# A softmax moved between two weight roundings, two late transposes and a store queue in an FFT filter + soft mixture + gated MLP kernel

## The chip, the cores and the metric

The kernel runs on one core of one Trainium2 chip. The metric is the device time of one execution in microseconds (us). The engines named below are TensorE (PE; PEld is its weight load), VectorE (DVE), ScalarE (ACT), GpSimd (POOL) and SyncE (SP). SP, ACT and POOL also issue DMAs (written SPq, ACTq, POOLq in the trace). Each engine runs its own instructions in program order, so an instruction that waits holds up everything behind it on that engine.

## The reference, cut to what matters

```python
X = np.fft.rfft(x, axis=1)                     # x: 8 x 3072 x 256
y = np.fft.irfft(X * (filt_r + 1j*filt_i)[None], n=3072, axis=1)   # -> 24576 tokens x 256
logits = y @ phi                               # 32 slots: 8 experts x 4
d = exp(logits - logits.max(0)); d /= d.sum(0) + 1e-09      # over all tokens
slot_input = (d.T @ y).reshape(8, 4, 256)
slot_out[e] = relu(slot_input[e] @ w1[e]) @ w2[e]           # F = 1024
c = exp(logits - logits.max(1)); c /= c.sum(1) + 1e-09      # over the 32 slots
z = c @ slot_out                               # 24576 x 256
g = z @ w_gate;  out = (g / (1 + exp(-g)) * (z @ w_val)) @ w_out    # hidden 1536
```

## The kernel before

**Three stages.** phase1 (0 to about 392 us of the profile) does the filter, the logits and the dispatch sums batch by batch; transition (to about 418 us) runs the eight experts on the 32 slots and multiplies the result into the gate and value weights; phase2 (to the end) walks 576 items, each of which makes G and V for 128 hidden units of 512 tokens (L964, L965), silu and product (L967, L973), a split into a rounded part and a remainder (L980, L981), and the projection to the output (L992, L996).

**Units of phase1.** A step is one half (128 of 256 channels) of one batch, so there are 16 steps; each has 6 units, written (step, u), 96 in all, numbered i. In a unit TensorE makes X (L258), DVE multiplies it by the filter into P and Q (L262, L263), POOL adds these into yt (L271, L273; the very last one on DVE). Two units later tail_ops transposes that yt through PSUM (T, L283, one buffer), and ACT copies it to y (L284); for odd u phi_pair multiplies two units by phi (L, L291), and DVE or ACT adds that to lts. For the next step s1_chunk makes s on TensorE (L230), DVE turns it (sg, L238), ACT spreads it into b (L247), which X reads.

**Chains.** When a batch is through, its generator chain(b) is advanced by pump once in each unit (twice in the last ten): transposes (L354), inverse transform (L364), a turn (L374), logits lg (L391, L398), store of the logits (L404), maximum, exponential (L422, L428), a second transform (L443, L455, L468) and the dispatch sum (L477). The chain of batch 7 (last) runs after the last unit with that of batch 6 (written g7 and g6), advanced by hand.

**Side work.** aside advances one list of generators, once or twice a unit: conv rounds the gate, value and output weights in 36 chunks (raw load L566, ACT L579 to L582, DVE L584, POOL L586 and L588, store L589), then first_weights makes the combining softmax of batch 0 in two halves G: load of the stored logits (lgf, L601), maximum (mx, L605), POOL subtraction (L606), exponential (L608), sum and reciprocal (sm, L611 to L613), POOL product (L614), turn (ctf, L617), rounding (chf, L620), remainder (L622), two stores to cd (L624). Its tiles and those of the raw weights are the same two buffers, taken in turn; half 1 can't load before a tile of half 0 has been stored. In phase2 build(b) does the same for batches 1 to 7 (L909 to L936).

**Queues.** Almost all loads and stores go out on SP in program order. A DMA of SP or ACT takes the next of eight semaphores (lanes; order calls them DMAHW0 to 7) and waits until the DMA eight before it has landed; those of POOL have lanes of their own (DMASW). While the last units run, the weights w1 are loaded by ACT's queue (L134), w2 by SP's (L743), then wv, the weights c4 (L891) and wo (L897).

**Ramp of phase2.** Item i makes G and V, then projects an item some places back. Up to item 11 load_out splits the output weights of one f: ACT copies a rounded part (L953), DVE subtracts the remainder (L954); proj of that f needs both. The gate and value weights for later f are put in place by 16 small DMAs (L871), half of them on POOL.

Of the kernel before, what the change touches and what calls it, by code (L numbers as in the profile page):

```python
# [12 lines left out]
ALU = mybir.AluOpType  # L13
# [4 lines left out]
NB, SEQ, D, E = 8, 3072, 256, 32  # L18
NEXP, SPE, FE, FF = 8, 4, 1024, 1536
NJ, NP, NR = 24, 96, 32  # L20
NF = FF // 128
# [4 lines left out]
CONV_AT = 14  # L26
# [53 lines left out]
def spectral_softmoe_glu_kernel(  # L80
# [17 lines left out]
    nc = tc.nc  # L98
    pe, dve, act, pool = nc.tensor, nc.vector, nc.scalar, nc.gpsimd
# [37 lines left out]
    def phase1():  # L137
        with ExitStack() as c1:
# [23 lines left out]
            yt = {}  # L162
            ytr = {}
# [108 lines left out]
                eng = dve if (step, u) == (2 * NB - 1, 5) else pool  # L272
                eng.tensor_tensor(out=y[:, :, 1, :], in0=Q[:, :, 0, :], in1=Q[:, :, 1, :], op=ALU.add)  # L273

            def tr_unit(step, u):
                b, h = divmod(step, 2)
                k = (6 * b + u - 6 * NB) % NY
                if h == 0:
                    yt[b, u] = yp[(k >= 2) + (k >= NY - 6)].tile([128, 4, D], F32, tag=f"y{k}", name="y")
                t = ytr[step, u // 2][:, u % 2].rearrange("p g r m -> p g (r m)")  # L280
                ps = ps_t.tile([128, 4, 128], F32, tag="T", name="T")
                for g in range(4):
                    pe.transpose(out=ps[:, g, :], in_=t[:, g, :], identity=ident)  # L283
                act.copy(yt[b, u][:, :, h * 128:(h + 1) * 128], ps)  # L284

            def phi_pair(step, q):
                b, h = divmod(step, 2)
                ps = ps_l.tile([128, 2, 128], F32, tag="L", name="L")
                t = ytr.pop((step, q)).rearrange("p u g r m -> p u g (r m)")
                for g in range(4):  # L290
                    pe.matmul(  # L291
                        out=ps[32 * g:32 * g + 32],
                        lhsT=phi_sb[:, h, :],
                        rhs=t[:, :, g, :],
                        tile_position=(0, 32 * g),
                    )
                if h == 0 and q == 0:
                    lts_t[b] = chp.tile([128, 3, 2, 128], F32, tag="lts", name="lts")
                dst = lts_t[b][:, q]
                if h == 0:  # L300
                    act.copy(dst, ps)
                else:
                    dve.tensor_tensor(out=dst, in0=dst, in1=ps, op=ALU.add)
# [4 lines left out]
            def chain(b, last):  # L308
# [92 lines left out]
                yield  # L401
                for h in range(2):
                    for g in range(2):
                        nc.sync.dma_start(  # L404
                            out=lgd[b].rearrange("(n h) g e k -> h g n e k", h=2)[h, g],
                            in_=lg[h][64 * g:64 * g + 48],
                        )
# [143 lines left out]
            def flat(a):  # L551
                return a.rearrange("(p a) f -> p (a f)", p=128)

            def conv():


                cw = 256
                chunks = [(i, c) for i in range(3) for c in range(FF * D // 128 // cw)]
                raws = {}

                def load(n):
# [86 lines left out]
                turn_filters(0, q)  # L648
            pool.tensor_scalar_mul(nyq, nyq, 0.5)
            dve.memset(expo, 0.0)  # L650
            side = [conv(), first_weights()]
            todo = []
            gens, ready = [], []
            units = [(s, u) for s in range(2 * NB) for u in range(6)]
# [16 lines left out]

            def tail_ops(i):
                if 0 <= i - 2 < len(units):
                    tr_unit(*units[i - 2])
                    s, u = units[i - 2]
                    if u % 2:
                        phi_pair(s, u // 2)
                    if s % 2 and u == 5:
                        ready.append((s // 2, chain(s // 2, s // 2 == NB - 1)))

            def aside():
                if next(side[0], 0) == 0 and len(side) > 1:
                    side.pop(0)

            for i, (s, u) in enumerate(units):
# [30 lines left out]
                    kept(1)  # L716
                if i == CONV_AT - 4 or i >= CONV_AT:
                    aside()
            wt = bp[1].tile([128, 3, FE], F32, tag="b", name="w")
            load_w1(nc.sync, 6, ((0, wt[:, 0]), (1, wt[:, 1])))  # L720
            load_w1(nc.sync, 7, ((1, wt[:, 2]),))
            for i in range(len(units), len(units) + 2):
                tail_ops(i)
            (_, g6), (_, g7) = gens + ready
            for g in (g7, g7, g7, g6, g7, g6, g7, g7, g6, g7, g6, g6):
                next(g, None)
            for _ in g7:
                pass
# [5 lines left out]
    def transition():  # L734
# [33 lines left out]
        for e in (6, 7, 0):  # L768
            load_w2(e)
        flat_load(wg, wd[0], 128)  # L770
        for e in (1, 2, 3, 5, 4):
            load_w2(e)
        flat_load(wv, wd[1], 128)

# [170 lines left out]
    def phase2(later):  # L945
# [5 lines left out]
        def load_out(f):  # L951
            st = wo[f][:, 1, :].bitcast(F32)
            act.copy(wo[f][:, 0, :], st)  # L953
            dve.tensor_tensor(out=wo[f][:, 1, :], in0=st, in1=wo[f][:, 0, :], op=ALU.subtract)  # L954

        items = [(b, q, G, f) for b in range(NB) for q in range(3) for G in range(2) for f in range(NF)]
        hb, hhi, hlo, acc, sb2 = {}, {}, {}, {}, {}
# [65 lines left out]
        for i in range(len(items) + LAG):  # L1023
            if i < len(items):
                b, q, G, f = items[i]
                if q == 0 and G == 0 and f == 0 and b:
                    for _ in gen:
                        pass
                    gen = build(b + 1) if b + 1 < NB else iter(())
                gv(i)  # L1030
            while todo and todo[0] <= i - lag(i):
                proj(todo.pop(0))
            if i < len(items):
                gate(i)
            if i < NF:
                load_out(i)
            if 0 <= i - 1 < len(items):
                split(i - 1)
            if i % 4 == 1:
                next(gen, None)  # L1040

    with tc.manual_schedule():
# [35 lines left out]
```

## Time and profile before

| | |
|---|---|
| median of three runs | 1502.65 us (1501.77, 1502.65, 1505.04) |
| the profiled execution | 1503.74 us |
| span of its trace | 1501.9 us (1.84 us of its time lie outside the span) |
| busy in the span | PE 1442.1, DVE 1158.6, ACT 962.7, POOL 232.9 us |

The times below are us from the start of the span. A row of the trace gives start, duration, engine, line, what is written and read, and in brackets the idle time of the engine before it and what ended that. The share of busy PE, 96%, is an average: phase2 and the middle of phase1 are nearly full, the last units of phase1 are not, so a change is to be read in the stage where it acts.

### The profile page before, as it was taken

How to read it: one execution, taken by the hardware profiler on the slowest of the kernel's cores; microseconds unless marked ns; L12 is line 12 of the kernel's file. 1: busy time of each engine (PE TensorE's matmuls, PEld its weight loads, DVE VectorE, ACT ScalarE, POOL GpSimd, SP SyncE). 2: the span in 40 equal slices, each digit the busy share in tenths (PEclk: the TensorE clock that was granted, in tenths of full speed). 3: DMA queues.
4: the chain of work that ended last, by engine and by line, in shares of the span. 5: the costliest groups of instructions: out<-in, count | busy, mean ns of one | idle time of the engine just before them, and what ended most of it. 6: DMA issues, size and time to landing. Idle time of an engine off the chain costs nothing.

```text
span 1501.9 us, 25182 instructions
## 1 busy us (share of the span) xinstructions
PE 1442.1 (96%) x9562; PEld 1152.8 (77%) x9562; DVE 1158.6 (77%) x1906; ACT 962.7 (64%) x1839; POOL 232.9 (16%) x299
## 2 busy tenths in 40 slices
PE   4899999986899999999999999999999999999998
PEld 2566666654468888888888888888888888888887
DVE  2788888874288878878887897888779778877775
ACT  2476666653277667766766776676676667666665
POOL 0466666652010000000000000000000000000000
PEclk9999999998999999999999999999999999999999
DMA  9978888855940310130121112111210310220011
GB/s 223 158 117 159 160 146 151 142 157 196 355 100 15 71 39 15 35 73 16 29 64 32 29 36 50 40 29 43 53 29 15 71 39 17 50 48 22 22 29 28
DMA packets 88248, 116.42 MB, mean 78 GB/s; under 512 B 8928, under 2 KB 65120, under 8 KB 88000
## 3 DMA queue, kind: packets, MB, share of 16 engines
q1 hardware_dynamic: 81072, 102.76, 31.6%
q10 hardware_dynamic: 6800, 11.54, 2.6%
q8 instruction: 75, 1.23, 0.4%
q0 software_dynamic: 256, 0.52, 0.2%
q14 instruction: 45, 0.37, 0.1%
HBM read 68.13 MB, written 34.60 MB: 68 GB/s over the span
## 4 chain that ended last, share of the span: by engine, by line
PE 85%; DVE 7%; DMA 4%; issue 2%; ACT 2%; POOL 0%; SPq 0%; ACTq 0%; DVEq 0%; POOLq 0%
PE o L992 35%; PE o L996 18%; PE V L965 9%; PE G L964 9%; PE X L258 4%; PE s L230 2%; PE T L283 2%; DVE sg L238 2%; PE c L477 1%; DVE Q L263 1%; DVE P L262 1%; PE L L291 1%; DMA wo<-wod 1%; DMA fraw<-in_filt_i_dram 1%; ACT b L247 1%
## 5 line engine op out<-in xcount | busy, mean ns | idle before, releaser
L992 PE MATMUL o<-wo,hi 128*128 128x512 f32 x2304 | 831.2, 395 | 0.0
L996 PE MATMUL o<-wo,lo 128*128 128x256 f32 x2304 | 644.6, 280 | 0.2 <-DVE lo L981 0.2
L967 ACT ACTIVATE s<-G 128x512 f32<-128x512 f32 x576 | 345.1, 599 | 318.1 <-PE G L964 314.6
L973 DVE TENSOR_TENSOR h<-V,s 128x512 f32<-128x512 f32 x576 | 395.0, 686 | 169.5 <-ACT s L967 168.8
L992 PEld LDWEIGHTS o<-wo,hi 128*128 128x128 f32 x2304 | 432.0, 187 | 103.4
L996 PEld LDWEIGHTS o<-wo,lo 128*128 128x128 f32 x2304 | 433.6, 188 | 25.9 <-DVE lo L981 0.6
L981 DVE TENSOR_TENSOR lo<-h,hi 128x512 fp32r<-128x512 f32 x576 | 417.1, 724 | 0.1
L980 ACT CAST hi<-h 128x512 fp32r<-128x512 f32 x576 | 354.7, 616 | 12.4 <-DVE h L973 9.1
L965 PE MATMUL V<-c,v 128*128 128x512 f32 x576 | 227.3, 395 | 1.9 <-DVE h L973 1.7
L964 PE MATMUL G<-c,g 128*128 128x512 f32 x576 | 228.0, 396 | 0.8 <-DMA g<-gl 0.6
L258 PEld LDWEIGHTS X<-fwd,b 128*128 128x128 f32 x768 | 97.1, 198 | 61.0 <-issue 41.2
L964 PEld LDWEIGHTS G<-c,g 128*128 128x128 f32 x576 | 108.1, 188 | 26.8 <-issue 1.1
L238 DVE STREAM_TRANSPOSE sg<-s 128x1024 f32<-128x1024 f32 x64 | 79.3, 1242 | 60.2 <-PE s L230 58.8
L258 PE MATMUL X<-fwd,b 128*128 128x128 f32 x768 | 113.7, 293 | 4.6 <-DVE Q L263 3.1
L965 PEld LDWEIGHTS V<-c,v 128*128 128x128 f32 x576 | 108.6, 189 | 3.7 <-DVE h L973 2.7
L911 POOL TENSOR_TENSOR lg<-lg,mx 96x1024 f32<-96x1024 f32 x7 | 16.9, 2418 | 581.8 <-DVE mx L909 581.8
L247 ACT COPY b<-sg 128x768 f32<-128x768 f32 x64 | 58.8, 922 | 67.4 <-DVE sg L238 67.3
L1006 DVE TENSOR_TENSOR ot<-o,tmp 128x256 f32<-128x256 f32 x192 | 70.1, 424 | 39.4 <-ACT tmp L1005 39.4
L230 PE MATMUL s<-x,csm 48*64 48x512 f32 x512 | 72.7, 628 | 22.7 <-DMA x<-in_x_dram 17.3
L271 POOL TENSOR_TENSOR yt<-P 128x256 f32<-128x256 f32 x96 | 70.2, 731 | 111.3 <-DVE P L262 110.0
L262 DVE TENSOR_TENSOR P<-X,ft 128x512 f32<-128x512 f32 x96 | 63.8, 665 | 12.2 <-PE X L258 11.7
L273 POOL TENSOR_TENSOR yt<-Q 128x256 f32<-128x256 f32 x95 | 71.1, 749 | 0.5
(197 smaller groups left out, 978.0 us busy)
## 6 DMA issues: line engine op xcount, KB each, us to landing
out_dram<-ot SPq DMA_DIRECT2D x192, 128.0 KB, 2.2
x<-in_x_dram SPq DMA_DIRECT2D x60, 384.0 KB, 8.2
w<-in_moe_w_dram SPq DMA_DIRECT2D x8, 1024.0 KB, 12.3
w<-in_moe_w_dram ACTq DMA_DIRECT2D x13, 512.0 KB, 6.0
c<-ch SPq DMA_DIRECT2D x42, 128.0 KB, 2.4
c<-cl SPq DMA_DIRECT2D x42, 128.0 KB, 2.5
raw<-in_moe_w_gate_dram SPq DMA_DIRECT2D x12, 256.0 KB, 5.4
lgd<-lg SPq DMA_DIRECT2D x32, 96.0 KB, 6.5
```

Of the source, the lines that this page charges most:

```text
L230: pe.matmul(out=ps[64 * k:64 * k + 64, 16 * r:16 * r + 16, :], lhsT=s1t_sb[64 * r:64 * r + 48, :], rhs=xt[step][64 * r:64 * r + 48, k, :, ...
L238: dve.transpose(out=sg.rearrange("p j d k -> p d j k"), in_=ps.rearrange("p n d -> p d n"))
L258: pe.matmul(out=ps[:, g].rearrange("p r m -> p (r m)"), lhsT=bb[:, j, :], rhs=fwd[:, j, :])
L262: dve.tensor_tensor(out=P, in0=ps, in1=f, op=ALU.mult)
L964: pe.matmul(out=pg, lhsT=g4[c][:, fs], rhs=c4[b][:, q, G, :])
L965: pe.matmul(out=pv, lhsT=v4[c][:, fs], rhs=c4[b][:, q, G, :])
L967: act.activation(s, pg, AF.Silu)
L973: dve.tensor_tensor(out=h, in0=pv, in1=s, op=ALU.mult)
L980: act.copy(hi, h)
L981: dve.tensor_tensor(out=lo, in0=h, in1=hi, op=ALU.subtract)
L992: pe.matmul(out=a, lhsT=hi[:, ts], rhs=wo[f].rearrange("p k d -> p (k d)"), start=(f == 0), stop=(f == NF - 1), skip_group_check=True,)
L996: pe.matmul(out=a[:, D:2 * D], lhsT=lo[:, ts], rhs=wo[f][:, 0, :], start=False, stop=(f == NF - 1), skip_group_check=True,)
```

## The change

Six edits, all in the order of things; the arithmetic is the same.

- The list of side work was conv (36 chunks), first_weights. It is now conv(0, 2) (24 chunks: gate and value), first_weights, conv(2, 3) (12 chunks: output).
- One aside more in units 0 and 3 of even steps from CONV_AT (i = 14) on.
- The transposes of units (15, 4) and (15, 5) leave tail_ops and go into the last chain, after its first and its second stage; their copies go to DVE.
- The last chain's four stores of logits are issued by POOL's queue.
- The w2 loads after wg come in the order 5, 4, 1, 2, 3 (before 1, 2, 3, 5, 4).
- load_out subtracts on POOL; build(1) starts at item 13 and no longer at item 1.

```diff
-                act.copy(yt[b, u][:, :, h * 128:(h + 1) * 128], ps)
+                copy(yt[b, u][:, :, h * 128:(h + 1) * 128], ps)
...
-                        nc.sync.dma_start(
+                        (nc.gpsimd if last else nc.sync).dma_start(
                             out=lgd[b].rearrange("(n h) g e k -> h g n e k", h=2)[h, g],
...
-            def conv():
+            def conv(first, end):
...
-                chunks = [(i, c) for i in range(3) for c in range(FF * D // 128 // cw)]
+                chunks = [(i, c) for i in range(first, end) for c in range(FF * D // 128 // cw)]
...
-            side = [conv(), first_weights()]
+            side = [conv(0, 2), first_weights(), conv(2, 3)]
...
                 if 0 <= i - 2 < len(units):
-                    tr_unit(*units[i - 2])
                     s, u = units[i - 2]
+                    if i < len(units):
+                        tr_unit(s, u)
...
                 if i == CONV_AT - 4 or i >= CONV_AT:
                     aside()
+                if i >= CONV_AT and s % 2 == 0 and u % 3 == 0:
+                    aside()
...
-            for g in (g7, g7, g7, g6, g7, g6, g7, g7, g6, g7, g6, g6):
+            next(g7)
+            for u in (4, 5):
+                tr_unit(2 * NB - 1, u, dve.tensor_copy)
+                next(g7)
+            for g in (g6, g7, g6, g7, g7, g6, g7, g6, g6):
                 next(g, None)
...
-        for e in (1, 2, 3, 5, 4):
+        for e in (5, 4, 1, 2, 3):
             load_w2(e)
...
-            dve.tensor_tensor(out=wo[f][:, 1, :], in0=st, in1=wo[f][:, 0, :], op=ALU.subtract)
+            pool.tensor_tensor(out=wo[f][:, 1, :], in0=st, in1=wo[f][:, 0, :], op=ALU.subtract)
...
-            if i % 4 == 1:
+            if i % 4 == 1 and i > NF:
                 next(gen, None)
```

How the instructions stand, in three places. In brackets is what a row waits for, a semaphore of an engine (its number here is always 49) or a DMA lane.

DVE before, from the end of the first half's softmax (unit (15, 0)) into the second half's, which stands among the units (15, 2) to (15, 5):

```order
L622 TENSOR_TENSOR ctf<-ctf,chf 96x512 [waits Activation_49]
L349 STREAM_TRANSPOSE bd<-c 128x512 [waits DMAHW2_49,DMAHW1_49,DMAHW7_49,DMAHW0_49,PE_49]
L349 STREAM_TRANSPOSE bd<-c 128x512
L262 TENSOR_TENSOR P<-X,ft 128x512 [waits PE_49,Pool_49]
L263 TENSOR_TENSOR Q<-X,ft 128x512 [waits Pool_49]
L605 TENSOR_REDUCE mx_4297<-lgf 96x16 [waits DMAHW1_49]
L262 TENSOR_TENSOR P<-X,ft 128x512 [waits PE_49,Pool_49]
L263 TENSOR_TENSOR Q<-X,ft 128x512 [waits Pool_49]
L611 TENSOR_REDUCE sm_4319<-lgf 96x16 [waits Activation_49]
L612 TENSOR_SCALAR sm_4319<-sm_4319 96x16 [waits DVE_49]
```

The change's DVE has no row of first_weights there; the two halves stand at i = 60 to 66, the second one from here (units (10, 4) to (11, 0)):

```order
L622 TENSOR_TENSOR ctf<-ctf,chf 96x512 [waits Activation_49]
L238 STREAM_TRANSPOSE sg<-s_2958 128x32x16x2 [waits PE_49]
L262 TENSOR_TENSOR P<-X,ft 128x512 [waits PE_49,Pool_49]
L263 TENSOR_TENSOR Q<-X,ft 128x512 [waits Pool_49]
L238 STREAM_TRANSPOSE sg<-s_3022 128x32x16x2 [waits PE_49,Activation_49]
L605 TENSOR_REDUCE mx_3029<-lgf 96x16 [waits DMAHW7_49]
L262 TENSOR_TENSOR P<-X,ft 128x512 [waits PE_49,Pool_49]
L263 TENSOR_TENSOR Q<-X,ft 128x512 [waits Pool_49]
L611 TENSOR_REDUCE sm_3053<-lgf 96x16 [waits Activation_49]
```

In both, the P and Q behind a row of the softmax wait with it; in the second place the turns sg of the next step (for s1_chunk) wait too.

SP of the change at the end of the moved softmax (cd its stores, raw the first two chunks of the output weights, lgd_75 the logits of batch 4):

```order
L601 DMA lgf<-lgd_71 96x512 [waits DMAHW7_49,DMAHW5_49,Pool_49]
L624 DMA cd<-chf 96x512 [waits DMAHW0_49,Activation_49]
L624 DMA cd<-ctf 96x512 [waits DMAHW1_49,DVE_49]
L178 DMA x<-in_x_dram 48x16x128 [waits DMAHW4_49,DMAHW2_49,PE_49]
L178 DMA x<-in_x_dram 48x16x128 [waits DMAHW3_49]
L404 DMA lgd_75<-lg 48x512 [waits DMAHW4_49,Activation_49]
L404 DMA lgd_75<-lg 48x512
L404 DMA lgd_75<-lg 48x512 [waits DMAHW6_49,Activation_49]
L404 DMA lgd_75<-lg 48x512 [waits DMAHW7_49]
L566 DMA raw<-in_moe_w_out_dram 128x512 [waits DMAHW0_49,Pool_49]
L566 DMA raw<-in_moe_w_out_dram 128x512 [waits DMAHW1_49]
```

Before, the chunks of conv followed each other without a break, each loaded two chunks ahead of its use; now the output weights start anew, their first raw load is the last thing of unit (11, 0), and ACT reads it (L579) in the middle of unit (11, 1).

PE before, around the end of phase1's units (T the transposes of (15, 4) and (15, 5), L354 the start of the last chain):

```order
L291 MATMUL L<-yt,phi_sb 32x256 [waits DVE_49]
L291 MATMUL L<-yt,phi_sb 32x256 x3
L283 MATMUL T<-csm,yt 128x128 [waits Activation_49,Pool_49]
L283 MATMUL T<-csm,yt 128x128 x3
L283 MATMUL T<-csm,yt 128x128 [waits DVE_49,Activation_49,Pool_49]
L283 MATMUL T<-csm,yt 128x128 x3
L291 MATMUL L<-yt,phi_sb 32x256 [waits DVE_49]
L291 MATMUL L<-yt,phi_sb 32x256 x3
L354 MATMUL cl<-csm,lts 128x128 x4
```

and of the change:

```order
L291 MATMUL L<-yt,phi_sb 32x256 [waits DVE_49,Pool_49]
L291 MATMUL L<-yt,phi_sb 32x256 x3
L354 MATMUL cl<-csm,lts 128x128 x4
L354 MATMUL cl<-csm,lts 128x128 [waits DVE_49]
L354 MATMUL cl<-csm,lts 128x128
L283 MATMUL T<-csm,yt 128x128 [waits Activation_49]
L283 MATMUL T<-csm,yt 128x128 x3
L364 MATMUL cl<-inv,lha 32x128 [waits Activation_49]
L364 MATMUL cl<-inv,lha 32x128 x15
L364 MATMUL cl<-inv,lhb 32x128 [waits DVE_49]
L364 MATMUL cl<-inv,lhb 32x128 x7
L283 MATMUL T<-csm,yt 128x128 [waits DVE_49]
```

The two T now stand where PE waits for ACT's and DVE's copies of the chain. On POOL, the first subtraction of wo, which the first projection needs, stands behind the eight DMA issues of L871; POOL's last four of these wait for lanes that the logits of batch 7 took before them.

## Rows read from the trace of the kernel before

**Rows 1.** By stretch: PE, PEld, DVE, ACT, POOL busy us (count); clock, DMA, GB/s.

```profile
255.00:265.00 10.00, 9.40 (x79) 5.24 (x79) 9.96 (x17) 7.14 (x13) 7.27 (x11) 1.00 1.18 197
317.00:362.00 45.00, 30.69 (x261) 20.37 (x260) 30.43 (x49) 16.70 (x31) 18.24 (x23) 0.91 0.49 174
335.30:339.30 4.00, 0.00 (x0) 0.00 (x0) 3.70 (x6) 1.76 (x4) 2.39 (x4) 1.00 0.01 2
339.30:343.50 4.20, 4.16 (x17) 2.45 (x18) 2.16 (x4) 1.49 (x3) 1.00 (x2) 0.61 0.80 286
364.00:367.80 3.80, 3.56 (x18) 2.06 (x18) 0.42 (x1) 0.69 (x3) 0.00 (x0) 0.53 0.89 348
460.00:1500.00 1040.00, 1036.54 (x5562) 887.64 (x5560) 833.28 (x1351) 711.15 (x1322) 31.26 (x13) 1.00 0.15 37
```

**Rows 2.** The chain that ended last, 317 to 420 us: start, us, what.

```profile
340.34 7.01 DMA cd<-chf
347.42 4.66 DMA lgf<-lgd
...
401.84 16.39 DMA wo<-wod
```

**Rows 3.** Busy time on tile lgf alone: DVE, ACT, POOL.

```profile
345.00:362.00 17.00, 3.07 (x3) 0.63 (x1) 2.52 (x2) 0.86 0.62 225
```

**Rows 4.** Busy time on tile chf alone: DVE, ACT.

```profile
345.00:362.00 17.00, 0.90 (x1) 0.62 (x1) 0.86 0.62 225
```

**Rows 5.** PE in order of time, at the ends of the last ten units.

```profile
316.50 1.16 PE L258 MATMUL X<-fwd,b 128*128 128x128 f32 x8
...
357.89 1.16 PE L258 MATMUL X<-fwd,b 128*128 128x128 f32 x8 [0.60 <-DVE Q L263]
360.47 0.88 PE L283 MATMUL T<-csm,yt 128*128 128x128 f32 x4 [1.41 <-ACT y L284]
...
364.12 1.09 PE L283 MATMUL T<-csm,yt 128*128 128x128 f32 x4 [0.72 <-issue]
...
366.15 1.53 PE L354 MATMUL cl<-csm,lts 128*128 128x128 f32 x6
```

**Rows 6.** PE, the dispatch sums (L477) of two chains, twelve units apart.

```profile
232.37 0.83 PE L477 MATMUL c<-y,dha 128*32 128x256 f32 x12
...
272.64 0.85 PE L477 MATMUL c<-y,dha 128*32 128x256 f32 x12
```

**Rows 7.** ACT in the tail.

```profile
347.78 0.59 ACT L284 COPY y<-T 128x512 f32<-128x512 f32 x1 [6.99 <-DMA cd<-chf]
```

**Rows 8.** Landing of the logits that first_weights loads (tile lgf, both halves).

```profile
DMA to landing us min/median/max: 4.7/5.3/5.9
```

**Rows 9.** DVE in the middle of phase1.

```profile
236.31 1.25 DVE L238 STREAM_TRANSPOSE sg<-s 128x1024 f32<-128x1024 f32 x1 [2.83 <-PE s L230]
```

**Rows 10.** DMA issues from 150 to 290 us: count, KB, median us to landing.

```profile
raw<-in_moe_w_out_dram SPq DMA_DIRECT2D x9, 256.0 KB, 4.8
lgd<-lg SPq DMA_DIRECT2D x12, 96.0 KB, 7.1
```

**Rows 11.** PE at the start of phase2.

```profile
420.88 0.40 PE L992 MATMUL o<-wo,hi 128*128 128x512 f32 x1
...
423.52 0.47 PE L964 MATMUL G<-c,g 128*128 128x512 f32 x1 [0.60 <-DMA g<-gl]
...
441.14 0.50 PE L965 MATMUL V<-c,v 128*128 128x512 f32 x1 [1.30 <-DVE h L973]
```

**Rows 12.** POOL at the start of phase2.

```profile
422.39 0.50 POOL L871 DMA_DIRECT2D v<-gl  x1
437.09 2.51 POOL L911 TENSOR_TENSOR lg<-lg,mx 96x1024 f32<-96x1024 f32 x1 [14.20 <-DVE mx L909]
```

**Rows 13.** DVE beside it.

```profile
437.52 2.36 DVE L954 TENSOR_TENSOR wo<-wo 128x256 fp32r<-128x256 f32 x1
```

**Rows 14.** The page's group for a POOL operation of 128x256.

```profile
L271 POOL TENSOR_TENSOR yt<-P 128x256 f32<-128x256 f32 x96 | 70.2, 731 | 111.3 <-DVE P L262 110.0
```

More of the change, by code (lines that the diff above doesn't have):

```diff
@@ L273, in s2_unit, with tr_unit @@
                 eng.tensor_tensor(out=y[:, :, 1, :], in0=Q[:, :, 0, :], in1=Q[:, :, 1, :], op=ALU.add)
-            def tr_unit(step, u):
+            def tr_unit(step, u, copy=act.copy):
                 b, h = divmod(step, 2)
@@ L288, in phi_pair @@
                 ps = ps_l.tile([128, 2, 128], F32, tag="L", name="L")
-                t = ytr.pop((step, q)).rearrange("p u g r m -> p u g (r m)")
+                t = ytr[step, q].rearrange("p u g r m -> p u g (r m)")
                 for g in range(4):
```

## The prediction

> **What bounds the kernel now.** I read busy time by stretch first. From 460 us on TensorE is busy 1036.5 of 1040 us [rows 1]: nothing that the change does can win there, and whatever it wins or loses ahead of the ramp moves the end by as much. From 317 to 362 us, the last ten units, TensorE is busy 30.69 of 45 us at a mean clock of 0.91 [rows 1]: that is the slack. The chain of waits says what holds it: a store of the softmax's first half, cd<-chf, 7.01 us to landing, then the load lgf for its second half, 4.66 us [rows 2]. After that the chain goes on through transition without a pause until wo is loaded and the ramp begins [rows 2]; wo's load is issued only when TensorE is through with w1, so time won in the tail should arrive in phase2 whole. Then I read the middle (222 to 265 us), where the softmax lands: from 255 to 265 us DVE is busy 9.96 of 10 us and TensorE 9.40 [rows 1]. There is little to hide anything under.
>
> **Softmax out of the tail.** One half costs DVE 3.07 us on lgf (maximum, sum, turn), 0.90 for the remainder and some 0.4 for the small steps (estimate), so 4.4; POOL 2.52; ACT 1.25 [rows 3, 4]. In DVE's order the P and Q of the units wait behind these rows, and with them X. Nine units, from X(14, 2) at 316.50 to X(15, 5) at 357.89, take 41.4 us [rows 5]. Undisturbed, twelve units take 272.64 - 232.37 = 40.3 us [rows 6], so nine take 30.2; the difference is 11.2. Not all of it returns: ACT issues the w1 loads in these units, and each waits for a lane; one such wait, 6.99 us, ended with cd<-chf's landing [rows 7]. That store is gone, but the loads' own landings take its place; I leave 1.3 us for it. Gain 9.9.
>
> **Two transposes later, and the end of the units.** From X(15, 5) to the end of L354 it is 366.15 + 1.53 - 357.89 = 9.8 us [rows 5]. Two T of about 1.09 leave (2.2; they go into waits of TensorE for the chain's copies), and with them the idle 0.72; the idle 1.41, ACT's y behind the rounding chf, leaves with the softmax [rows 5]. Of 360.47 to 367.68, what stays is 7.2 - 2.2 - 0.7 = 4.3 us at a granted clock near 0.53 [rows 1], the lower of the two levels (1.2 GHz) almost throughout. TensorE had stood idle often before that, as it had for 4 us at 335.3 before a stretch at 0.61 [rows 1]. With fewer gaps I give half of the 2.2 us back: 1.1. Sum 5.4. The copies on DVE stand ahead of nothing but the chain's own: 0.3 lost. Gain of the tail: 9.9 + 5.4 - 0.3 = 15.0. Bounds: 12.2 (no clock comes back, and the w1 loads cost 3 us), 16.3 (they cost nothing).
>
> The logits on POOL's queue and the w2 order take SP's queue out of the way of w2 and wg by under 2 us; these transfers are already at work when the experts need them, so I count nothing; w2_4 now waits for POOL's stores to land, and behind it stand the rest of w2 and wv (a rival below).
>
> **Softmax into the middle.** Four terms, each a delay of the engines in order.
> (1) First half. Its load is issued one unit (3.4 us) ahead of the maximum and lands after 5.3 [rows 8]: DVE waits 1.9 and works 4.4. In the trace DVE has 2.83 us idle there [rows 9]: 3.5 stays, of which the later, smaller idle times take back more than half: 1.8 (bounds 0 and 3.5).
> (2) Second half. Its load must wait for a store of the first half, 4.8 to land if it goes like raw's loads [rows 10], 7.0 as cd<-chf did [rows 2], then 4.7: 9.5 after the store's issue; two units of the order (6.7) lie between. DVE waits 2.8 (upper bound 6.2, with 7.0 and 5.9 [rows 2, 8]).
> (3) Second half's own 4.4 us on a DVE that is busy 9.96 of 10 [rows 1]: 4.4 on the path.
> (4) The output weights' first raw load is issued behind both last stores, two loads of x and four stores of lgd in SP's queue, and ACT needs it half a unit (1.7) later; it lands after 4.8 [rows 10]. ACT stops for 3.1 at least; with ACT stop y's copies, so T, so TensorE within a unit. The stores of lgd wait for the logits, which are late by (1) to (3) too, so that lateness doesn't hide the wait. With the queue ahead of it I replay ACT's stop at 8 us, 4 of which come on top of (1) to (3). Bounds: 0 where ACT is late itself, and 5.5 with transfers like lgd's 7.1 [rows 10].
> Sum 1.8 + 2.8 + 4.4 + 4.0 = 13.0. Nothing behind takes it back, since TensorE has no free time up to 317 us but the little above. Lower bound: (1) and (4) hidden, 2.8 + 4.4 = 7.2; upper: 3.5 + 6.2 + 4.4 + 5.5 = 19.6, and 1.6 more for a clock that falls after a gap (4.2 us at 0.61 [rows 1]). The extra asides only let conv end in time: their work existed before, and costs nothing new.
>
> **Ramp.** The first projection starts at 420.88 [rows 11]. It now needs a POOL subtraction, behind DMA issues that end at 422.39 + 0.50 [rows 12]; an operation of that size takes POOL 0.73 [rows 14]; so it starts at 423.6, 2.7 later. That swallows the idle 0.60 at 423.52 [rows 11]. It also takes away what made TensorE wait 1.30 at 441.14 [rows 11]: DVE's L954, 2.36 us at 437.52 beside POOL's L911 from 437.09 [rows 12, 13]. Net 2.7 - 0.6 - 1.3 = 0.8 lost (bounds: 0.5 gained, if DVE's twelve fewer operations take other small waits away; 3 lost).
>
> That L954 shows that a DVE and a POOL subtraction with both inputs in SBUF do not run side by side: the DVE one ended with POOL's. The Trainium skill says so too (SBUF — State Buffer, "SBUF: two separate sides": the two engines share one port pair, taken as an exclusive lock for a whole instruction), and its Perfetto Trace Analysis ("Optimizing Scalar/DVE Operations") warns that moving work between these two engines might therefore not help. By that rule the moved subtractions, 12 of 0.73 us, would each hold up DVE's split beside them, 8.8 us in all on DVE, less the 12 times 0.41 that it no longer does: an estimate from that page, and a rival below.
>
> **Sum.** -15.0 + 13.0 + 0.8 = -1.2 us against the profiled execution's 1503.74 (its span of 1501.9 and 1.84 around it), so 1502.5. That execution stands 1.1 above the median of the runs, 1502.65; against the median it is 1501.4. About 0.2%, 3 us, is what a measurement of this kernel can tell from no change; the forecast lies inside that: two large terms that nearly cancel.
>
> **Rivals.**
> A, faster: the middle absorbs most of it. For it: the engines have buffers to drift by a unit, and DVE's 2.83 us of idle time isn't the only one; against it: 9.96 of 10 behind it. If (4) hides and (1) is nothing, the middle costs 7.2 and the time is 1495.6. It decides when the raw load lands no later than ACT gets there.
> B, slower: the DMA legs of the moved softmax take the upper rows (7.0, 5.9, 7.1). x loads fill the queues in the middle, where the tail's were emptier; so it may well be. Then (2) is 6.2 and (4) 5.5: 4.9 us more, 1506.3. It decides (1505.7 is passed) from 4.3 us above my legs on.
> C, slower: the ramp with POOL's lock. If half of the twelve subtractions cost TensorE their full 0.73, that is 4.4 on top: 1505.8. Against it: DVE also loses 5 us of work, and phase2's order lets projections lag.
> D, slower: POOL's stores of the logits land late, w2_4 with all behind it on SP waits, and the experts' second product is late. wo is loaded 16.39 us under full DMA [rows 2]; 3 us of idle DMA engines would show there whole: 1504.4. Against it: the stores have the whole of the other w2 loads to land in.
>
> **How the numbers follow.** The forecast (its own range 1498.5 to 1504.5) has 0.42, A 0.33, B 0.15, C 0.06, D 0.04. Range: A's lower half leaves 1 in 10 below 1493, the upper bounds 1 in 10 above 1508. A lies below the 0.2% bound, 1499.6, and so does a tenth of the forecast's share: faster 0.37. Above 1505.7 lie B, half of C and the long ends of the rest: slower 0.23. Same 0.40.
>
> **What would show it.** In the trace after: X(15, 5) to the end of L354 about 4.4 us, no row of first_weights behind 280 us, and units (14, 2) to (15, 5) in 31 to 32 us; in the middle a DVE wait for lgf of 2 to 3 us twice, and an idle ACT of 3 to 8 us ahead of L579 that ended with DMA raw; the twelve units across it some 12 us longer than 40.3; the first projection 2 to 3 us behind V. I am wrong if ACT waits for no raw, if L954's successor stretches DVE's splits one after the other, or if stage2 waits for w2.

## The result, and the profile after

The changed kernel takes 1512.96 us (median of four runs, 1511.34 to 1513.45), the kernel before 1502.5 beside it: ratio 1.0065, interval 1.0047 to 1.0082. That is 9.8 us slower, where 1501.4 was forecast and 1508 was the upper end of the range. The profiled execution took 1512.8 us with a span of 1511.0, 9.1 more than that of before, so the spans below can be set side by side.

The two traces were laid over each other at marks that are the same instruction in both (X is L258 of a unit; positive is later than before):

| mark | before, us | after, us | later by |
|---|---|---|---|
| X(3, 5), last unit before the added asides bite | 104.47 | 102.52 | -1.95 |
| X(10, 0), the softmax begins | 228.41 | 235.93 | +7.52 |
| X(14, 1), middle over | 310.90 | 332.19 | +21.29 |
| X(15, 5) | 357.89 | 367.43 | +9.54 |
| end of L354 | 367.68 | 372.58 | +4.90 |
| first G of phase2 | 417.72 | 422.92 | +5.20 |
| end of the span | 1501.9 | 1511.0 | +9.1 |

So 9.5 us are lost ahead of the softmax, in a stretch where the prediction had nothing at all; 13.8 in the middle (forecast 13.0); 16.4 are won in the tail (forecast 15.0); 0.3 are lost in the last chain and transition, 3.9 in the ramp (forecast 0.8). The -1.95 at the first mark stands for the most part already at X(2, 0) (-1.80), ahead of the first additional aside, and differs from execution to execution. e3 below has the same code up to the ramp; its profiled execution gives 9.7, 16.3 and 12.6 us for the first three parts. So the 9.5 repeats, while the middle and the tail are each known to within 3 to 4 us only.

The stretch ahead of unit 60 answers to no row of before, since ACT waited for no raw load there. ACT's waits for raw in the trace after, 60 to 230 us (engine, instruction, what it waited for: us in total, times, longest), and the two largest pieces of the chain that ended last there (start, us, what):

```profile
ACT mag L579 <- DMA raw<-in_moe_w_gate_dram: 9.2, 3, 3.6
ACT mag L579 <- DMA raw<-in_moe_w_val_dram: 8.1, 6, 2.4
```

```profile
95.90 7.69 DMA raw<-in_moe_w_gate_dram
...
143.30 7.40 DMA raw<-in_moe_w_gate_dram
```

With three asides in a unit the four stages of a chunk follow each other faster, so the chunk two further on is wanted sooner after its load was issued. The fifth load of the gate weights, before (SP's issue, ACT's first use) and after (ACT's first use; its issue is the 95.90 above):

```profile
97.54 0.38 SPq L566 DMA_DIRECT2D raw<-in_moe_w_gate_dram  x1
104.72 0.46 ACT L579 ACTIVATE mag<-raw 128x256 f32<-128x256 f32 x1
```

```profile
103.67 0.43 ACT L579 ACTIVATE mag<-raw 128x256 f32<-128x256 f32 x1 [3.13 <-DMA raw<-in_moe_w_gate_dram]
```

Before, ACT takes it up 7.2 us after the issue; after, ACT is free for it after 4.6 us, and it has not landed. The landing itself has not become slower. All raw loads from 80 to 230 us, before and after:

```profile
DMA to landing us min/median/max: 3.0/5.0/7.3
DMA to landing us min/median/max: 2.7/4.1/7.7
```

What is shorter is the time from the issue to the moment ACT is free for the chunk: from the third chunk to the 24th its median is 7.2 us before and 4.9 after, its least 5.5 and 1.2. Where the load takes longer than that, ACT stops, behind it y's copy, and TensorE within a unit.

These waits are not the whole of the 9.5 us. X falls back by 5.7 us at (4, 0), (6, 0) and (8, 0) and the units just after, each time with an ACT wait of 2.4 to 3.6 us. But it falls back by 1.8 in the units (5, 2) to (5, 5), where ACT waits for no raw load, and by 2.2 from (9, 2) to (10, 0), with 1.8 us of such waits. Ahead of both places the added asides have moved two rounding operations of ACT (L581, L582) in front of its copy of the logits (lg, L398), and DVE waits longer for that copy than before (first row; then twice after):

```profile
130.54 1.28 DVE L399 TENSOR_REDUCE cm<-lg 128x32 f32<-128x512 f32 x2 [0.70 <-ACT lg L398]
132.93 1.28 DVE L399 TENSOR_REDUCE cm<-lg 128x32 f32<-128x512 f32 x2 [1.69 <-ACT lg L398]
217.03 1.28 DVE L399 TENSOR_REDUCE cm<-lg 128x32 f32<-128x512 f32 x2 [1.70 <-ACT lg L398]
```

DVE was busy 16.97 of 17.07 us from X(5, 1) to X(6, 0) before, so it has nothing to make up a delay with. That these waits of DVE make the other 4 us is read from the order of the rows; no run tests it.

The middle, in the trace after: the restart of the output weights on SP's queue, on ACT, and TensorE behind it, each in order of time.

```profile
265.66 0.30 SPq L624 DMA_DIRECT2D cd<-ctf  x1
266.07 1.04 SPq L178 DMA_DIRECT2D x<-in_x_dram  x2
267.20 1.91 SPq L404 DMA_DIRECT2D lgd<-lg  x4
269.21 1.08 SPq L566 DMA_DIRECT2D raw<-in_moe_w_out_dram  x2
```

```profile
275.63 0.43 ACT L579 ACTIVATE mag<-raw 128x256 f32<-128x256 f32 x1 [9.08 <-DMA raw<-in_moe_w_out_dram]
```

```profile
278.11 1.08 PE L283 MATMUL T<-csm,yt 128*128 128x128 f32 x4 [6.15 <-POOL low L588]
```

The load is issued behind the store, x and lgd as term (4) had it. ACT stands 9.08 us: 2.7 us until the load is even issued and 6.4 until it has landed. TensorE waits 6.15 us at once for POOL, whose additions stand behind that chunk. X(11, 3) is 12.8 us later than before and X(11, 5) 21.4, so 8.6 us are lost there. DVE, on the other hand, waits for neither load of the softmax's logits in this trace.

The tail and the ramp, answering to [rows 1]: busy time by stretch (PE, PEld, DVE, ACT, POOL; clock, DMA, GB/s).

```profile
340.00:369.00 29.00, 25.30 (x250) 17.08 (x252) 21.81 (x38) 15.68 (x31) 15.23 (x22) 1.00 0.60 215
367.60:372.60 5.00, 3.65 (x36) 2.34 (x36) 3.50 (x7) 1.17 (x2) 2.10 (x3) 1.00 1.03 401
428.00:432.00 4.00, 3.10 (x9) 2.68 (x10) 3.43 (x2) 0.36 (x1) 2.88 (x5) 0.50 0.87 216
432.00:436.00 4.00, 4.00 (x17) 3.35 (x16) 1.81 (x3) 2.35 (x6) 0.74 (x1) 0.74 0.00 1
462.00:1500.00 1038.00, 1037.03 (x5560) 887.57 (x5559) 836.18 (x1351) 715.67 (x1325) 33.66 (x14) 1.00 0.15 37
```

The last units are now fuller (25.30 of 29) and at the full clock, which holds to the end of L354, where it was 0.53; phase2 is as full as it was. But at 428 us, in the ramp, it is the lower level, 0.50. What the engine did before that, answering to [rows 11, 12]: PE's row and POOL's rows.

```profile
428.90 0.80 PE L999 MATMUL o<-wo,hi 128*128 128x512 f32 x1 [2.69 <-POOL wo L961]
```

```profile
427.59 0.50 POOL L878 DMA_DIRECT2D v<-gl  x1
428.11 2.79 POOL L961 TENSOR_TENSOR wo<-wo 128x256 fp32r<-128x256 f32 x4
```

TensorE waits 2.69 us for POOL's first subtraction behind its eight DMA issues, the 2.7 of the prediction; what the prediction left out is that the granted clock is the lower one after the gap, where the kernel before has 1.00 throughout its ramp (419 to 439 us).

### The profile page after: what moved, and what is told of

It is laid out like the page before. It is cut to its first block, busy times and chain, and to the rows that moved or that the text cites. A ratio compares the mean times of both kernels' runs of the same rounds, so it can differ in the third digit from the quotient of the medians.

```text
span 1511.0 us, 25184 instructions
## 1 busy us (share of the span) xinstructions
PE 1444.1 (96%) x9562; PEld 1153.5 (76%) x9562; DVE 1154.1 (76%) x1896; ACT 961.9 (64%) x1837; POOL 243.4 (16%) x315
## 4 chain that ended last, share of the span: by engine, by line
PE 82%; DVE 7%; DMA 4%; ACT 3%; issue 2%; POOL 1%; ACTq 0%; SPq 0%; DVEq 0%; POOLq 0%
PE o L999 35%; PE o L1003 18%; PE V L972 9%; PE G L971 9%; PE X L258 3%; PE s L230 2%; DVE sg L238 2%; DMA raw<-in_moe_w_gate_dram 1%; PE T L283 1%; DVE P L262 1%; DVE Q L263 1%; PE c L477 1%; DMA fraw<-in_filt_i_dram 1%; PE L L291 1%; DMA raw<-in_moe_w_out_dram 1%
## 5 line engine op out<-in xcount | busy, mean ns | idle before, releaser
L988 DVE TENSOR_TENSOR lo<-h,hi 128x512 fp32r<-128x512 f32 x576 | 422.3, 733 | 1.1
L987 ACT CAST hi<-h 128x512 fp32r<-128x512 f32 x576 | 354.6, 616 | 11.5 <-DVE h L980 8.2
L258 PEld LDWEIGHTS X<-fwd,b 128*128 128x128 f32 x768 | 95.8, 196 | 59.1 <-issue 40.3
L258 PE MATMUL X<-fwd,b 128*128 128x128 f32 x768 | 112.1, 290 | 2.4 <-ACT b L247 1.3
L1012 ACT COPY tmp<-o 128x256 f32<-128x256 f32 x192 | 68.0, 374 | 4.3 <-PE o L1003 4.3
```

The costliest lines, as they stand in the source:

```text
L258: pe.matmul(out=ps[:, g].rearrange("p r m -> p (r m)"), lhsT=bb[:, j, :], rhs=fwd[:, j, :])
L987: act.copy(hi, h)
L988: dve.tensor_tensor(out=lo, in0=h, in1=hi, op=ALU.subtract)
```

## The experiments

Twelve kernels, each timed against before on the same chip. Executions of one kernel scatter by 2 to 10 us here (before: 1498.97 to 1509.64), so a kernel is judged by its ratio, and a mechanism by marks in the trace; each trace is one execution, which may lie at either end of its kernel's scatter. "G to end" is the time from the first G to the end of the span; before 1084.2, after 1088.1.

| kernel | median, us | ratio to before (interval) | G to end, us |
|---|---|---|---|
| changed kernel | 1512.96 | 1.0065 (1.0047 to 1.0082) | 1088.1 |
| e1, no additional asides | 1507.06 | 1.0032 (1.0022 to 1.0043) | 1087.2 |
| e2, before + additional asides | 1515.45 | 1.0074 (1.0054 to 1.0095) | 1083.4 |
| e3, changed, subtraction on DVE | 1510.49 | 1.0039 (1.0019 to 1.0058) | 1084.0 |
| e4, before + new list of side work | 1508.55 | 1.0037 (1.0022 to 1.0052) | 1084.9 |
| e5, before + edits of the tail | 1499.79 | 0.9970 (0.9958 to 0.9982) | 1083.9 |
| e6, list + tail | 1503.76 | 1.0000 (0.9986 to 1.0014) | 1083.4 |
| e7, list + tail + pause | 1506.75 | 1.0019 (1.0008 to 1.0031) | 1083.8 |
| e8, e7 + logits loaded sooner | 1501.39 | 0.9980 (0.9967 to 0.9993) | 1083.8 |
| e9, list + tail, side work from unit 6 | 1498.39 | 0.9974 (0.9962 to 0.9987) | 1084.4 |
| e10, e8's waits, side work from unit 4 | 1496.88 | 0.9959 (0.9945 to 0.9974) | 1084.4 |
| e11, e5, side work from unit 6 | 1495.12 | 0.9949 (0.9936 to 0.9962) | 1083.5 |
| e12, e11 + logits loaded sooner | 1495.16 | 0.9939 (0.9926 to 0.9953) | 1083.8 |

**e1: the additional asides undone.**

```diff
-                if i >= CONV_AT and s % 2 == 0 and u % 3 == 0:
-                    aside()
```

> The changed kernel without the additional asides in units 0 and 3 of even steps. Theory (the asides shorten the way from a raw load to its use, ACT waits for the raws of the gate and value weights, 17.3 us in nine waits, and X(10, 0) comes 9.3 us later than it would): those waits go, X(10, 0) is back at 228 to 229, and the time is about 1512.8 - 9.3 = 1503.5; up to 2 us of it may be lost again, because the rounding of the output weights then ends in the very last units. Rival (the asides are free, as the prediction said; the lateness ahead of unit 60 has another cause): 1511 to 1513.5, X(10, 0) near 236.

X(10, 0) is at 227.50, 0.9 before that of before and 8.4 before that of the changed kernel. ACT's waits for raw from 60 to 230 us shrink from 17.3 to 1.3:

```profile
ACT mag L579 <- DMA raw<-in_moe_w_gate_dram: 0.7, 1, 0.7
ACT mag L579 <- DMA raw<-in_moe_w_val_dram: 0.6, 2, 0.4
```

The whole is only 5 us faster than the changed kernel by the ratios, though, and at 1507.06 above the 1503.5 to 1505.5 expected: part of the gain is lost again in the tail (e6 to e9).

**e2: the asides alone, on the kernel before.**

```diff
+                if i >= CONV_AT and s % 2 == 0 and u % 3 == 0:
+                    aside()
```

> The kernel before with the additional asides alone. Theory: ACT waits for raw loads between 60 and 230 us, where it waited for none; X(10, 0) at 236 to 238. The rounding ends sooner, so the softmax moves some units forward (out of part of the tail), which gives a part back: 1505 to 1511. Rival (asides free): X(10, 0) at 228 to 229 and 1495 to 1502.5.

Here nothing else is changed, and the kernel is slower than before by 11 us by the ratio; its median is 4.5 us above the range expected. X(10, 0) is at 236.91, and ACT waits for the raws of gate and value weights again:

```profile
ACT mag L579 <- DMA raw<-in_moe_w_gate_dram: 8.2, 4, 2.7
ACT mag L579 <- DMA raw<-in_moe_w_val_dram: 8.2, 6, 2.7
```

With e1 this settles that the asides make the 9.5 us. By which waits is shown in part only: X falls back by 1.9 us in the units (5, 2) to (5, 5) here too, as in the changed kernel, and at (6, 0) and (6, 1) by 1.3 with no raw wait at all. Not all that e2 loses lies ahead of X(10, 0) either: its softmax stands in units 83 to 89, and its first G follows the end of L354 by 55.0 us, where it was 50.0; a load of wv, 25.62 us to landing, is on the chain there.

**e3: the ramp's subtraction back on DVE.**

```diff
-            pool.tensor_tensor(out=wo[f][:, 1, :], in0=st, in1=wo[f][:, 0, :], op=ALU.subtract)
+            dve.tensor_tensor(out=wo[f][:, 1, :], in0=st, in1=wo[f][:, 0, :], op=ALU.subtract)
```

> The changed kernel with load_out's subtraction back on DVE. Theory (the first projection waits 2.7 us for POOL's first subtraction behind the eight DMA issues, and the clock that falls after that gap costs some 2 us more, less 1 for a DVE wait that the move avoids): about 3.9 us less, 1509. Rival (DVE's relief is worth as much as the wait): 1512 to 1513.5.

The ratio falls by 0.0026, 3.9 us, as expected; the two intervals overlap, so the ramp's own time decides: from the first G to the end it takes 1084.0 us, as before (1084.2) and not 1088.1. So POOL's subtraction costs 4 us in the ramp. (In its profiled execution the middle took longer than in the changed kernel's, with X(13, 0) 3.8 us further back by the same code; the part from the first G on is not touched by that.)

**e4: the new list of side work alone.**

```diff
-            side = [conv(), first_weights()]
+            side = [conv(0, 2), first_weights(), conv(2, 3)]
```

> The kernel before with the new order of side work alone (gate and value weights, softmax, output weights); no other edit. Theory: the middle costs 13 to 14 us (two waits of DVE for the softmax's loads, 4.4 us of work twice, ACT's wait for the first raw of the output weights), the units of the tail give 13 back, and 2 to 3 of the 4.6 us at the units' end: 1500 to 1503. Rival (the middle absorbs the softmax once the asides are not in its way): 1490 to 1495.

1508.55, above both. The middle costs 11.5 us (X(14, 1) is 10.1 later than that of before, where X(10, 0) was 1.4 earlier), less than expected. But the tail gives only 7.9 of it back: the end of L354 is still 2.1 later than that of before, and the first G follows it by 52.6 us instead of 50.0. The gain that the theory gave to the units of the tail doesn't follow from the move alone.

**e5 and e6: the edits of the tail, without and with the new list.** e5 is before with the two late transposes, the logits on POOL's queue and the w2 order; e6 has the new list too; neither has the additional asides or the changed ramp.

```diff
 e5, against the changed kernel
-            side = [conv(0, 2), first_weights(), conv(2, 3)]
+            side = [conv(0, 3), first_weights()]
...
 e5 and e6, against the changed kernel
-                if i >= CONV_AT and s % 2 == 0 and u % 3 == 0:
-                    aside()
...
-            pool.tensor_tensor(out=wo[f][:, 1, :], in0=st, in1=wo[f][:, 0, :], op=ALU.subtract)
+            dve.tensor_tensor(out=wo[f][:, 1, :], in0=st, in1=wo[f][:, 0, :], op=ALU.subtract)
...
-            if i % 4 == 1 and i > NF:
+            if i % 4 == 1:
```

> The kernel before with the edits of the tail alone: two late transposes, the last logits on POOL's queue, the w2 order. Side work, asides and ramp are as before. Theory (these three are worth what the two earlier runs differ by at the first G of phase2: 415.9 with them, 422.4 without, both with the moved softmax and without more asides): 6 us faster than before, 1496.5. Rival (they pay only where the softmax has left the tail; with it there, its chain of store and load bounds the units and the transposes hide anyway): 1501 to 1502.5.

> The changed kernel without the additional asides and with the ramp of before (subtraction on DVE, build(1) from item 1): moved softmax and the edits of the tail. Theory: the run without the asides stood 4.8 us above before, of which POOL's subtraction in the ramp was 3 to 4: 1503 to 1504.5, no difference that can be told from before. Rival (the asides and POOL's subtraction are not all; the softmax in the middle costs more than the tail gives back): 1506 or more.

The edits of the tail are worth 4.5 us by themselves; 6 was expected. With the softmax moved between the weights there is nothing left of that: ratio 1.0000, as expected. So the move itself, without the asides, costs 4.5 us (e6 against e5; e4 alone 5.6). Part of the reason is in the last units, as e8's trace shows below.

**e7 and e8: the waits of the middle.** e7 lets the output weights' rounding rest two units between load and use; e8 also loads each half's logits two units ahead of the maximum. To make room, side work starts two and four units earlier (CONV_AT 12 and 10).

```diff
 e7 and e8, against e6
                 load(1)
                 yield
+                if first:
+                    for _ in range(4):
+                        yield
...
 e8 alone
                     nc.sync.dma_start(out=lg, in_=lgd[0][:, G])
-                    yield
-                    yield
+                    for _ in range(4):
+                        yield
```

> As the list-and-tail kernel, and the output weights' rounding pauses two units between its first raw loads and their use; side work begins two units earlier to make room. Theory (ACT's wait for the first raw is on the path, term 4 of the prediction: X(11, 4) lies 5.3 us later than X(11, 3) does): 3 to 5 us less than the list-and-tail kernel. Rival (ACT's wait only takes the place of DVE's delay, which comes out anyway): less than 1 us.

> As the kernel with the pause, and each half's logits are loaded two units ahead of the maximum instead of one; side work begins two units earlier still. Theory (DVE's waits for these loads, about 3.5 us in all, are on the path, terms 1 and 2): 2 to 4 us less than with the pause alone. Rival (what costs is DVE's 4.4 us of work for each half, which stays): no difference.

e7 is not faster than e6 but 3 us slower by the medians. The rest alone moves the delay: from X(10, 0) to X(12, 0) the middle loses 11.7 us in e7 and 11.3 in e6, since in e7 ACT no longer waits for raw, but the first half's logits take 8.47 us to land and hold DVE for 3.74 (e6: 0.92), and the delay of DVE comes out in full. That the wait for raw is worth 3 to 5 us by itself has fallen; where e7 loses its 3 us is not shown, since e6's trace is of one of its slowest executions (1507.27, median 1503.76). With both waits taken away (e8) the same stretch loses 8.0, and the kernel is 0.4% faster than e7: together they are on the path. (e8's side work also starts two units sooner than e7's; its gain in the last units, below, is about the same.)

In e4, e6, e7 and e8 the rounding of the output weights now runs to the last units, beside the w1 loads. In e8's trace its last raw load takes 8.82 us to land (the chain that ended last: start, us, what; then the busy time of the stretch that follows, in the order of the columns above):

```profile
352.26 8.82 DMA raw<-in_moe_w_out_dram
```

```profile
357.50:362.50 5.00, 0.27 (x2) 0.30 (x3) 0.85 (x3) 1.31 (x4) 0.80 (x2) 0.68 0.58 222
```

ACT waits 6.40 us for it, TensorE stands for almost five us, and the five us after that run at the lower clock (0.50). From X(14, 3) to the end of L354 e4, e6, e7 and e8 win 7.6 to 8.8 us over before, e1 12.3 (e1 and e6 have the same code up to there, so 3.5 us of this are scatter); the changed kernel, whose additional asides have ended the rounding by then, wins 17.9. That is what the asides buy: they cost 9.5 us and give 6 to 10 back.

**e9 and e10: end the rounding early without more asides.** All side work starts at unit 6 (e9), or at unit 4 with the rests of e8 (e10); the first subtraction of wo is on DVE, the other eleven are on POOL, and build(1) starts at item 13 as in the changed kernel.

```diff
-CONV_AT = 14
+CONV_AT = 6
...
-                if i >= CONV_AT and s % 2 == 0 and u % 3 == 0:
-                    aside()
...
-            pool.tensor_tensor(out=wo[f][:, 1, :], in0=st, in1=wo[f][:, 0, :], op=ALU.subtract)
+            (pool if f else dve).tensor_tensor(out=wo[f][:, 1, :], in0=st, in1=wo[f][:, 0, :], op=ALU.subtract)
```

> The changed kernel without the additional asides; instead all side work begins eight units earlier (unit 6), so that it ends as early as with them; and load_out's first subtraction on DVE, the other eleven on POOL. Theory (the asides cost 8 to 9 us by the raw waits and give 6 to 9 back by ending the rounding before the w1 loads of the last units; POOL's cost in the ramp is the first subtraction alone): no ACT wait for raw up to 200 us, the gain of the tail is that of the changed kernel (17.9 us, against 8 to 9 in the list-and-tail kernel), and from the first G to the end it takes 1083 to 1084 us, as with DVE alone (the changed kernel: 1088.1). Time 1497 to 1500. Rival (the asides' cost is in the work itself, wherever it lies; or the other eleven subtractions cost by the shared port): 1503 or more, or over 1086 from the first G.

> As the kernel with early side work, with the pause of two units ahead of the output weights' first use and the logits' loads two units ahead of the maximum; side work begins ten units earlier than in the changed kernel. Theory (the waits of terms 1, 2 and 4 are on the path and add up to some 8 us): 4 to 8 us less, 1490 to 1495. Rival (DVE's work is what costs): within 1 us of the kernel with early side work.

e9 behaves nearly as expected. X(9, 0) is 1.2 earlier than that of before, with 2.2 us of raw waits up to 205 us, where none was expected; from X(14, 3) to the end of L354 it wins 18.3; from the first G it takes 1084.4 us with eleven of the twelve subtractions on POOL; the time is in its range. So the ramp's cost was the first subtraction alone, and the other eleven on POOL cost next to nothing. At the end of the units, answering to the 0.53 of [rows 1]:

```profile
357.00:362.00 5.00, 3.65 (x36) 2.34 (x36) 3.59 (x7) 1.17 (x2) 2.10 (x3) 1.00 1.02 392
```

e10 wins 5.4 us in the middle (its stretch from X(9, 0) to X(12, 5) loses 5.5 us, that of e9 11.0), but starts so early that ACT waits 5.9 us for raw beside the first loads, so that little of it is left: 1.5 us by the medians, within the intervals of both, and short of the 1490 to 1495 expected.

**e11 and e12: the softmax stays behind the weights, everything earlier.** e11 is e5 with CONV_AT = 6; e12 also loads the logits two units ahead, as e8 does.

> The tail-only kernel (order of side work and ramp of before) with all side work eight units earlier, so that the softmax is through before the last units without being put between the weights. Theory (what the tail wants is only that all side work is through; the restart of the output weights, term 4, doesn't arise): the softmax costs 8 to 9 us at units 78 to 86 and gives 13 or more back: 3 to 6 us less than the tail-only kernel, 1494 to 1497. Rival (the place in the middle is what helps): no less than the tail-only kernel's 1499.8.

> The tail-only kernel with early side work, and each half's logits loaded two units ahead of the maximum instead of one. Theory (in the kernel with early side work DVE waits 6.5 us for the second half's load, and the step from X(13, 3) to X(13, 5) is 9.7 us longer; the wait is on the path): 4 to 6 us less, 1489 to 1491. Rival (DVE's work takes the place of the wait): 1494 to 1495.

e11 and e12 are the fastest kernels: 0.9949 and 0.9939, 7.7 and 9.2 us faster than before, with intervals that overlap. e11 is as expected. The softmax now lies at units 78 to 86; e11's X(14, 3) is 11.0 later than that of before, and the end of the units gives all of it and more back. In e12 X(14, 2) comes 4.4 us sooner than in e11, but the end of L354 is the same, and so is the median. The time is the rival's, its mechanism is not: the wait that was taken away did come out, and the 4.4 us were lost later. In e12's trace the granted clock is 0.92 on the mean from 340 us to the end of L354, in e11's 1.00; what else holds these units was not followed up.

## Why the prediction was wrong

**The step that failed** is "The extra asides only let conv end in time: their work existed before, and costs nothing new". The work did exist, but the asides changed its pace against its loads and its place among the other work. They cost 9.5 us by X(10, 0) in the changed kernel, 8.4 against e1; e2 shows them alone, 8.4. The cover that the step took for granted, two chunks of distance between load and use, is counted in asides and not in us, and the added asides shorten it; these waits go with 5.7 of the 9.5, and what makes the rest is argued only. With it, the forecast would have been 8.4 to 9.5 us above 1501.4, and with the ramp's 3 us (below) 1513 to 1514. None of the prediction's three signs of being wrong looked at this stretch.

By the timed ratios the way from the kernel before to the changed one is: edits of the tail -4.5 us (e5), the new list +4.5 (e6), the ramp +4.8 (e1), the asides +5.0, with what they give back in the last units already taken off. Each step is uncertain by 2 to 3 us.

**Softmax into the middle: right in sum by luck, wrong in its parts.** 13.8 us for 13.0 in this execution; 16.3 in e3's by the same code, and 11.2 to 13.2 without the asides (e1, e4, e6). X(10, 0) to X(10, 5) lost 1.3 (term 1: 1.8); up to X(11, 3) it was 4.0 (terms 2 and 3: 7.2); the raw load cost 8.6 on top (term 4: 4.0). The waits of DVE for the logits, 1.9 and 2.8 in terms 1 and 2, did not come at all in this trace (in e1 the second is 3.43). The total came out because the delays ahead of the raw load were smaller and its own larger; e7 shows that they trade against each other.

**Tail: right in mechanism, its size not settled.** From X(14, 2) to X(15, 5) it won 12.6 (9.9 forecast; 7.9 in e3's execution), from there to the end of L354 4.6 (5.4 - 0.3). The clock came back altogether, where half was counted. The condition that the prediction did not name is that the rounding of the output weights must be out of the last units: without the asides a third (e1) to over half (e6 to e8) of the gain is gone, and with all side work started early it is there without them (18.3 in e9 and in e11).

**Edits counted at nothing.** The logits on POOL's queue and the w2 order were put at nothing; with the two transposes they are worth 4.5 us (e5). How that divides between them was not tried. Rival D did not come: the first G follows the end of L354 by 50.0 us before and 50.3 after.

**Ramp: the wait right, the consequence missed.** 2.69 us for 2.7; but after the gap TensorE ran at 1.2 GHz, 0.50 from 428 to 432 us and 0.74 on the mean of the next four. TensorE's waits in the 52 us from the first G add up to 2.9 us before and 3.6 after, so the 0.8 was right for the waits. The two stretches at the lower clock give up 2.0 and 1.0 us of full speed (an estimate from 0.50 and 0.74 of 4 us), which is the rest. The prediction had such a term for the middle, as an upper bound, and none here. Net 3.9 for 0.8; e3 gives 4.1 back.

**Rivals.** A had the wrong sign. B had the right sign, but its legs did not come: the first half's stores landed after 4.4 us at most, the second half's load after 2.3 and the raw load after 6.4, where B asked for 7.0, 5.9 and 7.1. C, the shared port, fell with e9: eleven subtractions on POOL and 1084.4 us from the first G. The lock itself is there, as the Trainium skill says (SBUF — State Buffer, "SBUF: two separate sides"). In the trace after it stretches one split of DVE (its remainder, L988) to 3.05 us beside POOL's first four subtractions, eight more to about 0.81, and one to 2.51 beside build's POOL operation, where 0.68 is the rule. So the prediction's sign, DVE's splits stretched one after the other, did come; but TensorE waited only 0.9 us for DVE in the 52 us from the first G:

```profile
428.40 3.05 DVE L988 TENSOR_TENSOR lo<-h,hi 128x512 fp32r<-128x512 f32 x1
468.27 2.51 DVE L988 TENSOR_TENSOR lo<-h,hi 128x512 fp32r<-128x512 f32 x1
471.31 0.68 DVE L988 TENSOR_TENSOR lo<-h,hi 128x512 fp32r<-128x512 f32 x1
```

```profile
467.83 2.40 POOL L918 TENSOR_TENSOR lg<-lg,mx 96x1024 f32<-96x1024 f32 x1 [20.43 <-DVE mx L916]
```

## What to carry to other kernels

A prefetch distance that is counted in steps of a schedule is a time only as long as the steps keep their pace: whoever adds steps for more room shortens every such distance, so compare it with the longest landing of the load, not with its median. Added steps also change which operations of other work they stand in front of; look where the engine behind them has no slack. When work is moved out of a stage with slack, look also at what the move pushes into that stage in its place: here the weights' rounding ran into the last units, and starting all side work earlier (e11) did more than the new order did. A wait on the path of TensorE is to be priced with the clock after it; here 2.7 us of waiting cost 4.

## What the runs showed of the hardware that was not expected

The wait of 2.69 us, in a stretch in which TensorE was busy 1.88 of 4 us (424 to 428), was followed by a clock of 0.50 and 0.74 in the next two stretches of 4 us; in e1, with about the same wait (2.67), by 0.63 and 0.94. These are also the two executions that took longest from the first G (1088.1 and 1087.2 us; all others 1083.4 to 1084.9). And raw loads of the same 256 KB landed in 3.0 to 7.3 us within one stretch of the kernel before (80 to 230 us, median 5.0); those on the chain that ended last took 7.4 and 7.7 us in the changed kernel ahead of the softmax, and 8.8 in e8's last units.
